# k of batch 0 in one transfer in place of two halves, in a fused attention and maxout feed-forward kernel

## The chip, the core and the metric

The kernel runs on one NeuronCore of a Trainium2 chip. The metric is the device time of one execution in microseconds (us); the median of several executions is compared. The core has five engines with instruction queues of their own: TensorE (PE, with its weight loads shown as PEld), VectorE (DVE), ScalarE (ACT), GpSimd (POOL) and SyncE (SP). Transfers between HBM and the on-chip memory run on 16 DMA engines that all queues share. A transfer that casts float32 to bfloat16 is issued by POOL here, and goes through one queue, which the profile calls software_dynamic.

## What is computed

For 8 batches and 8 heads, with sequence length 576, head size 64 and 32 memory slots:

```python
a = exp(phi - max over s); a = a / sum over s
k_m = einsum('bhsm,bhsd->bhmd', a, k)
v_m = einsum('bhsm,bhsd->bhmd', a, v)
scores = q @ k_m^T / 8
attn = softmax(scores)
x = (attn @ v_m), heads joined: 4608 x 512
h = maximum(maximum(x @ w1, x @ w2), x @ w3)     # 512 -> 768
out = h @ w_out                                  # 768 -> 512, float32
```

All inputs are float32 in HBM; the kernel computes in bfloat16.

## The kernel before

One batch is handled as four pairs of heads (index j, 0 to 3). A load of k, v or q of a batch puts 128 partitions x 4 pairs x 576 elements into a tile: 576 KB in bfloat16, 512 rows of 1152 bytes each, one for each partition and pair. The stages of a batch b are: the exponential of phi (E), the products of that with k and v over the sequence (B, L249, into PSUM), a normalization and transposition of the small result (N and K, L269 to L304), the scores against the transposed q (Q at L313, S at L333), the softmax, and then the feed-forward part. The feed-forward weights are folded with each batch's v_m (D, L440), so that the kernel multiplies the folded weights by the attention (F, L466), takes the maxima, and multiplies by w_out (T, L497 and L506). For that it once needs the product of w3 and w_out: W transposes w3 (L184), and O multiplies it by w_out (L192).

The order of everything is written out by hand, in one string of tokens (L594 on) that `issue` (L561) turns into calls: `X@b` is stage X of batch b. Each engine and each queue gets its instructions in the order of the string. The tokens that matter here:

- `E@0`: the two exponentials of batch 0, on ACT. Their input phi is loaded by SP in two transfers, ahead of the string (L91).
- `L1@b`, `L2@b`, `L3@b`: k, v, q of batch b, each in one transfer issued by POOL (L97 and L110). `L0@b`: phi of a later batch (L93).
- `H0@b` to `H3@b`: half of k or v, two pairs of heads in one transfer (L97 too). `H0` is k of pairs 0 and 1, `H2` k of pairs 2 and 3, `H1` and `H3` the same for v.
- `Y0@0` to `Y3@0`: the weights w1, w2, w3 (L116) and w_out (L123).
- `Z25@0`, `Z9@0`, `Z2@0`, `Z6@0`: so many matrix products on zeros (L159), whose results nobody reads.
- `B0@0`: the products with k of batch 0. Its 72 matmuls run over c (9 positions), j (4 pairs) and two heads, with c outermost, so the first eight read all four pairs.
- `B1@0`: the products with v of batch 0, read straight from the loaded tile.

POOL's transfers of batch 0 are issued in this order: k of pairs 2 and 3, k of pairs 0 and 1, q, w3, w_out, v in two halves, w1, w2; then phi, k, q and v of batch 1. The completion of POOL's transfers is counted on eight semaphores in rotation, so the ninth transfer is issued only when the first has landed, the tenth only when the second has, and so on: w2 waits for the first half of k, phi of batch 1 for the second half, k of batch 1 for q, q of batch 1 for w3, and v of batch 1 for w_out.

The load in question, with `h` the slice of the pairs:

```python
    def load_kv(b, i, h=slice(0, NP)):
        kv = loaded.setdefault(b, {})["kv"] = kvos[b % 2]
        nc.gpsimd.dma_start(
            out=kv[:, 1 - i, h].rearrange("p j c d -> p j (c d)"),
            in_=by_pair((k, v)[i], b)[:, h],
        )
```

Of the kernel before, what the change touches and what calls it, by code (L numbers as in the profile page):

```python
# [15 lines left out]
def kernel(  # L16
# [14 lines left out]
    B, H, S, D = q.shape  # L31
# [529 lines left out]
    def issue(b, n, swap):  # L561

        i = int(n[1:]) if len(n) > 1 else None
        {
            "I": lambda: [make_identity(nc, ident)]
            + [nc.gpsimd.memset(x[:, :, :, 2 * D : 2 * D + 1], 1.0) for x in kvrs],
            "Y": lambda: load_w(i) if i < 3 else load_wo(),
            "L": lambda: load_ph(b) if i == 0 else load_q(b) if i == 3 else load_kv(b, i - 1),
            "H": lambda: load_kv(b, i % 2, halves[i // 2]),
            "r": lambda: pack(b, i),  # L570
            "E": lambda: [att_exp(b, h) for h in (halves if b == 0 else [slice(0, NP)])],
            "B": lambda: att_kv(b, i),
            "N": lambda: att_kv_norm(b, i),
            "K": lambda: att_kv_t(b, swap, i),
            "Q": lambda: att_q(b, i),
            "S": lambda: att_score(b),
            "a": lambda: att_t(b, i),
            "s": lambda: att_sum(b, i),
            "c": lambda: att_rec(b, i),
            "m": lambda: att_mul(b, i),  # L580
            "X": lambda: (ones_mul if (b, i) in ONES else att_back)(b, i),
            "M": lambda: ones_sum(b, i),
            "R": lambda: ones_rec(b, i),
            "D": lambda: fold(b, i, swap),
            "F": lambda: ffn1(b, i, swap),
            "T": lambda: ffn2(b, i, swap),
            "W": lambda: w3_t(i, swap),
            "O": lambda: w3_o(i, swap),
            "V": lambda: w_diff(i),
            "Z": lambda: warm_up(i),  # L590
        }[n[0]]()


    for w in """  # L594
        E@0 H2@0 H0@0 L3@0 Z25@0 B0@0 I@0 N0@0 Z2@0 K0@0! Q0@0 Q1@0 Z9@0 S@0 Z2@0 M0@0 M1@0
        R0@0 Y2@0 R1@0 W0@0 Y3@0 W1@0 W2@0 Z6@0 O1@0 H3@0 O3@0 O2@0 H1@0 X1@0 B1@0 X0@0 N1@0
        K1@0 O0@0 Y0@0 D1@0! D0@0! D3@0 F8@0 F10@0 F2@0 V0@0 F6@0 F0@0! Y1@0 D2@0 D4@0 F4@0
        L0@1 V1@0 F1@0 E@1 F3@0 L1@1 F5@0 F9@0 F7@0 L3@1 F11@0 B0@1 T3@0 N0@1 K0@1! L2@1 Q1@1
        L2@2 L1@2 Q0@1 L0@2 V2@0 T0@0! L3@2 S@1 T1@0 a0@1 s0@1 c0@1 m0@1 B1@1 N1@1 a1@1 L1@3
        K1@1 s1@1 D0@1 D1@1! D2@1 c1@1 m1@1 X0@1 L3@3 r1@2 X1@1 T2@0! L2@3 F6@1 F10@1 F7@1 F2@1  # L600
        F3@1 F4@1 F0@1 r0@2 E@2 F5@1 F1@1 F11@1 L0@3 L0@4 F8@1 L2@4 F9@1 B@2 D3@1 N@2 Q1@2
        T0@1! K@2 T2@1! r0@3 Q0@2 S@2 a0@2 a1@2 s1@2 c1@2 m1@2 T4@1! D1@2! s0@2 D2@2 c0@2 m0@2
        X1@2 D0@2 T3@1 Q0@3 L3@4 X0@2 Q1@3 T1@1 F0@2 F4@2 F8@2 F6@2 F9@2 E@3 F7@2 r1@3 F5@2
        F10@2 F1@2 B@3 L1@4 D3@2 N@3 L0@5 F2@2 F11@2 E@4 F3@2 L1@5 K@3 r1@4 L2@5 T2@2! S@3 T3@2
        a0@3 s0@3 c0@3 m0@3 D0@3 D2@3 a1@3 s1@3 c1@3 X0@3 D1@3! Q0@4 m1@3 T1@2 L3@5 L2@6 T0@2!
        X1@3 F10@3 r0@4 F2@3 F4@3 E@5 Q1@4 r0@5 F5@3 F3@3 L1@6 F8@3 B@4 N@4 D3@3 F9@3 F6@3
        F11@3 L0@6 K@4 F0@3 F7@3 F1@3 S@4 a0@4 T4@3! s0@4 a1@4 D0@4 c0@4 s1@4 r1@5 c1@4 D3@4
        m0@4 X0@4 Q0@5 T0@3! D1@4! D2@4 B@5 T3@3 m1@4 X1@4 L0@7 F10@4 Q1@5 N@5 F8@4 K@5 F6@4
        F9@4 S@5 F7@4 L3@6 F2@4 F4@4 a0@5 L1@7 a1@5 F0@4 s0@5 r1@6 F3@4 D0@5 r0@6 s1@5 c1@5 E@6
        D3@5 m1@5 c0@5 F1@4 T1@3 L2@7 F11@4 L3@7 E@7 F5@4 m0@5 B@6 D1@5! D2@5 X1@5 N@6 T2@3!  # L610
        X0@5 F6@5 F8@5 Q0@6 Q1@6 K@6 F4@5 F9@5 S@6 F7@5 r0@7 a0@6 F2@5 a1@6 s0@6 c0@6 F0@5
        F10@5 m0@6 F1@5 s1@6 c1@6 F11@5 F5@5 T0@4! F3@5 X0@6 T2@4! r1@7 D0@6 D1@6! Q0@7 B@7
        m1@6 N@7 X1@6 T2@5! K@7 T3@4 Q1@7 S@7 a0@7 F2@6 s0@7 a1@7 s1@7 c1@7 m1@7 c0@7 F4@6
        T4@5! D3@6 D2@7 D0@7! T0@5! D3@7 D2@6 X1@7 m0@7 D1@7! T1@4 X0@7 F6@7 F3@6 T1@5 F4@7
        F8@7 F0@7 F5@6 F10@6 F7@7 F9@7 F10@7 F5@7 F0@6 F11@7 F6@6 F1@7 F7@6 F2@7 F8@6 F11@6
        F9@6 F1@6 F3@7 T0@6! T0@7! T3@5 T2@7! T2@6! T1@6 T1@7 T3@6 T4@7! T3@7
    """.split():
        n, b = w.rstrip("!").split("@")
        issue(int(b), n, w.endswith("!"))
# [30 lines left out]
```

## Time and profile before

| what | value |
|---|---|
| time, median of 3 runs | 165.75 us (165.37 to 166.11) |
| time of the profiled execution | 164.78 us |
| its span, first to last instruction | 163.0 us |
| PE busy | 152.5 us (94%) |
| ACT, DVE, POOL busy | 100.5, 90.3, 69.6 us |
| granted TensorE clock, mean | 0.998 |
| moved by the software_dynamic queue | 21.43 MB, 68.7% of 16 engines' span |
| two half loads of k, issue to landing | 7.0 us (median) |

The span is the time from the first to the last instruction of one profiled execution; about 1.8 us of the execution's own time lie around it. In the windows of the profile, "DMA share" is the mean busy share of the 16 DMA engines (it passes 1 where packets of one engine overlap), and GB/s is what they moved, counted in bytes at the destination. In the chain of waits, each piece is followed back to what released it, so a stretch marked DMA is one in which the end of the kernel hung on a transfer from its issue to its landing.

### The profile page before, as it was taken

How to read it: one execution, taken by the hardware profiler on the slowest of the kernel's cores; microseconds unless marked ns; L12 is line 12 of the kernel's file. 1: busy time of each engine (PE TensorE's matmuls, PEld its weight loads, DVE VectorE, ACT ScalarE, POOL GpSimd, SP SyncE). 2: the span in 40 equal slices, each digit the busy share in tenths (PEclk: the TensorE clock that was granted, in tenths of full speed). 3: DMA queues.
4: the chain of work that ended last, by engine and by line, in shares of the span. 5: the costliest groups of instructions: out<-in, count | busy, mean ns of one | idle time of the engine just before them, and what ended most of it. 6: DMA issues, size and time to landing. Idle time of an engine off the chain costs nothing.

```text
span 163.0 us, 4818 instructions
## 1 busy us (share of the span) xinstructions
PE 152.5 (94%) x2060; PEld 85.4 (52%) x2080; DVE 90.3 (55%) x181; ACT 100.5 (62%) x151; POOL 69.6 (43%) x71
## 2 busy tenths in 40 slices
PE   7968798999899999999999999999999999999990
PEld 2433444664377436744673575576553467744450
DVE  2013703898838575848499658879749128810010
ACT  4204435935497488778876899994558976223320
POOL 7931215100699268548849967656403100000000
PEclk9999999999999999999999999999999999999999
DMA  5999999999999999999999999997313130014333
GB/s 154 153 199 208 206 210 212 279 207 209 259 311 237 208 251 373 283 209 286 260 264 206 234 347 270 195 237 157 129 73 126 68 129 0 0 69 186 135 129 131
DMA packets 21974, 31.77 MB, mean 195 GB/s; under 512 B 1216, under 2 KB 16576, under 8 KB 21952
## 3 DMA queue, kind: packets, MB, share of 16 engines
q0 software_dynamic: 16080, 21.43, 68.7%
q1 hardware_dynamic: 5728, 9.90, 17.2%
q8 instruction: 16, 0.26, 0.6%
q10 hardware_dynamic: 144, 0.13, 0.2%
q14 instruction: 6, 0.05, 0.1%
HBM read 39.32 MB, written 9.44 MB: 299 GB/s over the span
## 4 chain that ended last, share of the span: by engine, by line
PE 83%; DMA 9%; POOL 2%; issue 1%; ACT 1%; DVE 1%; POOLq 0%; ACTq 0%
PE psum L466 30%; PE psum L497 28%; DMA wo_sb<-in_moe_w_out_dram 9%; PE psum L506 8%; PE psum L440 5%; PE psum L249 4%; PE psum L192 3%; PE psum L333 2%; PE psum L515 1%; POOL kvo L97 1%; PE psum L298 1%; PE psum L538 1%; POOL qq L110 0%; DVE kvn L273 0%; ACT w3o L172 0%
## 5 line engine op out<-in xcount | busy, mean ns | idle before, releaser
L497 PE MATMUL psum<-wo_sb,hT 128*128 128x512 bf16 x193 | 49.7, 380 | 1.4 <-issue 0.6
L466 PE MATMUL psum<-attn,wp 128*128 128x288 bf16 x384 | 50.5, 286 | 0.1
L479 DVE TENSOR_TENSOR hT<-psum,h 128x576 bf16<-128x576 f32 x48 | 34.2, 749 | 17.5 <-PE psum L466 12.0
L466 PEld LDWEIGHTS <-wp 128*128 128x128 bf16 x384 | 36.7, 98 | 13.2 <-issue 2.0
L172 ACT COPY ot<-psum 128x512 f32<-128x512 f32 x35 | 20.7, 591 | 32.2 <-PE psum L506 25.2
L497 PEld LDWEIGHTS <-hT 128*128 128x128 bf16 x210 | 19.2, 98 | 24.1 <-issue 4.3
L172 ACT CAST wp<-psum 128x1024 bf16<-128x1024 f32 (+1 forms) x31 | 29.3, 996 | 3.3 <-PE psum L440 1.5
L103 POOL COPY kvr<-kvo 128x2304 bf16<-128x2304 bf16 x12 | 25.4, 2116 | 13.7 <-DMA kvo<-in_k_dram 10.2
L170 ACT ACTIVATE h<-psum 128x576 bf16<-128x576 f32 x47 | 28.4, 660 | 3.5 <-PE psum L466 3.3
L409 POOL TENSOR_TENSOR t<-t,sm 128x576 bf16<-128x576 bf16 x14 | 16.1, 1156 | 24.6 <-DVE sm L404 24.5
L506 PE MATMUL psum<-wp,attn 128*128 128x512 bf16 x62 | 18.4, 379 | 0.0
L159 PE MATMUL psum<-warm 128*128 128x512 bf16 x42 | 12.0, 438 | 1.4 <-DVE warm L128 1.2
L313 DVE STREAM_TRANSPOSE qT<-qq 128x576 f32<-128x576 f32 x16 | 11.7, 746 | 1.2 <-DMA qq<-in_q_dram 1.1
L342 ACT ACTIVATE e<-psum 128x576 bf16<-128x576 f32 x16 | 9.6, 652 | 3.7 <-PE psum L333 3.7
L229 ACT ACTIVATE e<-ph 128x1152 bf16<-128x1152 f32 (+1 forms) x9 | 9.6, 1068 | 1.8 <-DMA ph<-in_phi_dram 1.7
L395 DVE TENSOR_REDUCE sm<-t 128x18 f32<-128x576 bf16 x14 | 10.3, 737 | 0.2
L387 DVE STREAM_TRANSPOSE t<-e 128x288 f32<-128x288 f32 x14 | 6.4, 464 | 6.3 <-ACT e L342 6.2
L97 POOL DMA_DIRECT2D kvo<-in_v_dram x9 | 6.7, 751 | 7.2 <-PE psum L249 4.1
L506 PEld LDWEIGHTS <-attn 128*128 128x128 bf16 x62 | 6.1, 98 | 7.1
L555 DVE COPY ot<-psum 128x256 f32<-128x256 f32 x1 | 0.4, 425 | 15.4 <-PE psum L546 15.4
L249 PEld LDWEIGHTS <-e 64*32 64x32 bf16 x720 | 6.9, 90 | 3.6 <-issue 3.2
L110 POOL DMA_DIRECT2D qq<-in_q_dram x8 | 6.2, 770 | 6.0 <-DMA w_sb<-in_moe_w_dram 6.0
(57 smaller groups left out, 114.4 us busy)
## 6 DMA issues: line engine op xcount, KB each, us to landing
out_dram<-ot SPq DMA_DIRECT2D x35, 256.0 KB, 5.5
qq<-in_q_dram POOLq DMA_DIRECT2D x8, 576.0 KB, 12.7
ph<-in_phi_dram POOLq DMA_DIRECT2D x7, 576.0 KB, 14.4
kvo<-in_k_dram POOLq DMA_DIRECT2D x7, 576.0 KB, 14.1
kvo<-in_v_dram POOLq DMA_DIRECT2D x7, 576.0 KB, 15.8
w_sb<-in_moe_w_dram POOLq DMA_DIRECT2D x3, 768.0 KB, 19.2
wo_sb<-in_moe_w_out_dram POOLq DMA_DIRECT2D x1, 768.0 KB, 14.9
ph<-in_phi_dram SPq DMA_DIRECT2D x2, 288.0 KB, 3.1
```

The source lines that it names most:

```text
L103: nc.gpsimd.tensor_copy(out=kvrs[b % 2][:, :, :, D * i : D * (i + 1)], in_=kvos[b % 2][:, 1 - i])
L159: nc.tensor.matmul(po[:, 0:BANK], lhsT=warm[:, 0:P], rhs=warm, start=True, stop=True)
L170: nc.scalar.activation(out=out_, in_=in_, func=AF.Relu)
L172: nc.scalar.copy(out=out_, in_=in_)
L249: nc.tensor.matmul(kvp[M * j : M * (j + 1), a, 0:nd], lhsT=s["e"][r, j, c, :], rhs={None: lambda: kvr[r, j, c, 0:nd], 0: lambda: k_and_one ...
L313: nc.vector.transpose(out=s["qT"][:, j].rearrange("p j c r e -> p (j c r e)").bitcast(FP32), in_=loaded[b]["q"][:, j].rearrange("p j c d - ...
L395: nc.vector.tensor_reduce(out=sm, in_=s["t", g].rearrange("p n r e -> p n e r"), op=ALU.add, axis=mybir.AxisListType.X,)
L409: nc.gpsimd.tensor_tensor(out=t, in0=t, in1=s["sm", g].unsqueeze(2).to_broadcast([P, S // HP, R, 2]), op=ALU.mult,)
L466: nc.tensor.matmul(acc[:, h, 0:SH], lhsT=wps[b][:, g, w * DF + ft * P : w * DF + (ft + 1) * P], rhs=attn[:, g, c0 : c0 + SH], start=(g == ...
L479: nc.vector.tensor_tensor(out=hT[:, ft, (b % 2) * S : (b % 2 + 1) * S].rearrange("p (h n) -> p h n", h=2), in0=a, in1=s["h1", ft], op=ALU.max,
L497: nc.tensor.matmul(po, lhsT=hT[:, fc, c0 : c0 + P], rhs=wo_sb[:, fc, :], start=(n == 0), stop=False,)
L506: nc.tensor.matmul(po, lhsT=attn[:, g, c0 : c0 + P], rhs=wp3s[b][:, g, :], start=False, stop=(g == NG - 1),)
```

## The change

One line of the string of tokens. The two half loads of k of batch 0 are replaced by the load of the whole, at the same place:

```diff
     for w in """
-        E@0 H2@0 H0@0 L3@0 Z25@0 B0@0 I@0 N0@0 Z2@0 K0@0! Q0@0 Q1@0 Z9@0 S@0 Z2@0 M0@0 M1@0
+        E@0 L1@0 L3@0 Z25@0 B0@0 I@0 N0@0 Z2@0 K0@0! Q0@0 Q1@0 Z9@0 S@0 Z2@0 M0@0 M1@0
         R0@0 Y2@0 R1@0 W0@0 Y3@0 W1@0 W2@0 Z6@0 O1@0 H3@0 O3@0 O2@0 H1@0 X1@0 B1@0 X0@0 N1@0
```

`L1@0` calls `load_kv(0, 0)` with all pairs, `H2@0` and `H0@0` called it with pairs 2 and 3, then 0 and 1. The same 512 rows go to the same places. POOL has one transfer fewer; the other engines have the same instructions in the same order. The rotation of the eight semaphores moves by one: w2 no longer waits for a landing, phi of batch 1 waits for the whole of k, and every later transfer waits for the same earlier transfer as before.

## The prediction

> **What bounds the kernel now.** I read the chain of waits first, in order of time, for the opening 30 us, since the change touches only the opening:
>
> ```profile
> 1.25 0.89 POOL kvo L97
> ...
> 2.15 0.70 POOL kvo L97
> 2.85 0.76 POOL qq L110
> ...
> 5.01 14.86 DMA wo_sb<-in_moe_w_out_dram
> ...
> 19.92 4.04 PE psum L192 x18
> ```
>
> The columns are start, length and what. Up to 19.9 us the end of the kernel hangs on w_out landing; it is issued at 5.01 and takes 14.86 us because it stands in the queue behind k, q and w3. Then PE takes over, and the whole-run shares of the chain (PE 83%, DMA 9%, the 9% being this one wait) say that it keeps the chain to the end. The timeline of PE shows what stands ahead of that point:
>
> ```profile
> 9.54 0.80 PE L249 MATMUL psum<-kvo,e 64*32 64x128 bf16 x72 [0.72 <-DMA kvo<-in_k_dram]
> ...
> 17.62 1.24 PE L159 MATMUL psum<-warm 128*128 128x512 bf16 x5
> 19.92 4.04 PE L192 MATMUL psum<-wo_sb,w3T 128*128 128x512 bf16 x18 [1.05 <-DMA wo_sb<-in_moe_w_out_dram]
> ```
>
> PE waits 0.72 us for k at 9.54, but that wait is not on the path: everything between 9.5 and 18.9 is filled with products on zeros, and PE then stands 1.05 us for w_out. So k may land a little earlier or later at no price. What counts is when the queue has brought w_out, and that is read from the stream of the DMA engines in windows of half a microsecond (the last three columns: granted clock, DMA share, GB/s):
>
> ```profile
> 3.50:4.00 0.50, 0.50 (x3) 0.15 (x1) 0.00 (x0) 0.28 (x1) 0.42 (x3) 1.00 1.12 334
> 4.00:4.50 0.50, 0.50 (x2) 0.15 (x1) 0.00 (x0) 0.43 (x2) 0.50 (x4) 1.00 1.18 173
> 4.50:5.00 0.50, 0.50 (x2) 0.15 (x1) 0.00 (x0) 0.50 (x1) 0.50 (x2) 1.00 0.95 159
> 5.00:5.50 0.50, 0.50 (x3) 0.23 (x2) 0.00 (x0) 0.15 (x1) 0.50 (x2) 1.00 1.29 143
> 5.50:6.00 0.50, 0.50 (x4) 0.22 (x3) 0.00 (x0) 0.00 (x0) 0.50 (x2) 1.00 0.76 81
> 6.00:6.50 0.50, 0.50 (x4) 0.20 (x2) 0.00 (x0) 0.00 (x0) 0.50 (x1) 1.00 0.97 122
> 6.50:7.00 0.50, 0.50 (x4) 0.26 (x3) 0.00 (x0) 0.00 (x0) 0.50 (x2) 1.00 1.09 175
> ...
> 8.00:8.50 0.50, 0.50 (x4) 0.20 (x2) 0.00 (x0) 0.00 (x0) 0.28 (x2) 1.00 1.14 168
> ```
>
> Until 4 us the stream is phi (uncast, 320 to 334 GB/s), then k. Between 5.0 and 6.5 it falls to 81 GB/s and recovers. The packet records of the trace place this: on most of the 16 engines the first half of k is through between 5.25 and 5.8, and the first packets of the second half take 0.3 to 1.3 us where the usual one takes 0.11. The dip lies on the seam between the two transfers that the change joins.
>
> **The change part by part.**
>
> POOL: two issues of 0.89 and 0.72 us (2.85 - 1.25 = 1.60 together) give way to one. What a whole load of k or v costs is in the rows of the same line:
>
> ```profile
> L97 POOL DMA_DIRECT2D kvo<-in_k_dram x4: 722/746/885, 1.2 to 25.7; - x4
> ```
>
> About 0.75 us, so q, the identity, w3, w_out and all up to w1 are issued some 0.85 us earlier. Worth nothing by itself: w_out is issued at 5.01 and its packets can start only when w3 is through, on the fastest engine at 14.3 by the packet records, so 9 us of backlog cover it. Were the cover gone, it would be worth its whole 0.85 us.
>
> The semaphore rotation: w2, issued at 8.26 after 0.22 us of waiting for the first half of k, waits for nothing and is issued about 1.1 us earlier. Its last packets come at 29.9, over 21 us after the issue, so this is worth nothing either. The next in POOL's queue, phi of batch 1, waits for the end of k as before; behind it stand the loads of batch 1, each waiting for the transfer it waited for before. If k lands earlier they follow, into a queue that has a backlog anyway.
>
> The seam: if the dip goes away, the whole stream behind it moves up. Take 170 GB/s as its undisturbed rate here (between the 159 and 173 ahead of the dip and the 175 behind it): the three windows from 5.0 to 6.5 miss 27, 89 and 48 GB/s over 0.5 us each, 82 KB, which at 170 GB/s is 0.48 us. By 159 GB/s they miss 65 KB, or 0.41 us. I take 0.45 us as the size of the dip. How much of it comes back? In the one whole transfer whose predecessors had nearly run dry (v of the last batch, issued at 101.85, its first packets at 103.9) there is a slack stretch too:
>
> ```profile
> 103.50:104.00 0.50, 0.50 (x17) 0.11 (x2) 0.50 (x2) 0.50 (x2) 0.50 (x1) 1.00 1.27 205
> 104.00:104.50 0.50, 0.45 (x3) 0.25 (x3) 0.47 (x4) 0.50 (x1) 0.50 (x1) 1.00 1.17 175
> ```
>
> So a seam behind which the next transfer was issued only 2 us earlier costs something (about 0.27 us there, 175, 171 and 171 GB/s in three windows against some 207 around them: 52 KB at 207, or 0.25 to 0.27 with 205 to 212). The seam from k to q, where q was issued 4.5 us ahead, shows only the 168 between 187 and 184 GB/s: under 0.06 us. After the change the seam from k to q is the only one left in the opening, with q issued at 2.0 and due at about 7.2, a lead of 5 us. I therefore let nearly all of the 0.45 us come back, and set 0.4.
>
> The start of the stream: the first packet of k starts at 3.60, 2.35 us after the issue of the half at 1.25. No row shows the start of a whole load on an idle queue, so it is bounded. From below: v of the last batch above had its first packets 2.1 us after its issue with no gap behind the transfer ahead of it, so twice the rows need not take longer; and the 3.60 is the moment at which the first DMA engine is done with phi, so an earlier readiness gains at most the share of phi's own bandwidth that k would take, which is nothing in sum. From above: if the first packet waits until all 512 rows are described, and the second 256 cost what the second issue cost, it starts 0.72 us later. I take the nearer row, 746 against 722 ns, which is 0.03 us later.
>
> The Trainium skill has two rules that pull apart here. "DMA: Bandwidth & Descriptors", section "Anatomy of one DMA - SWDGE (gpsimd) path", gives a fixed cost of about 2.0 us for each DMA; taken as serial, the change would gain 2.0 us, but the row of the seam has room for no more than 0.48, so most of a fixed cost is overlapped here. The same page, section "Queues, rings and completion order", says that a DMA engine takes turns between the queues it has work for, packet by packet; this speaks against the change, since by it k's packets would have mixed with phi's before 3.60 had they been ready, so that the start would hang on k's descriptors and not on phi, and a larger transfer could be late by the 0.72 us of the bound.
>
> The sum: -0.40 (seam) + 0.03 (start) + 0 (POOL) + 0 (rotation) = -0.37 us on w_out's landing. PE's wait of 1.05 us ahead of L192 has room for it (the third copy of w3T ends at 18.68, the last product on zeros at 18.86). Behind it v, w1 and w2 come from the same stream and move with it, and PE, which has hardly any idle time from there on, carries the shift to the end one for one. The profiled execution would go from 164.78 to 164.41 (span 163.0 to 162.6). The median of the runs is 0.97 us above the profiled execution; from 165.75 the same step gives 165.4.
>
> **The rivals.**
>
> - A, the forecast: the seam's dip goes, 0.2 to 0.6 us, 165.15 to 165.55. Chance 0.38. For it: the place of the dip. Against: the records show slow packets also on engines whose first half was late, which no seam explains.
> - B, the dip is not the seam's but the opening's (cold descriptors, phi and POOL's writes in the same time), and stays where it is. The change then does nothing on the path: 165.75, within 0.2. Chance 0.25. For it: the seam from q to w3 shows no slow packet at all.
> - C, slower: the start is late. One mechanism, at the head of the queue: all 512 rows must be described before the first packet goes. Price up to 0.72 us, and the dip's slow first packets then stay in the opening as well, so w_out lands up to 0.7 later and PE's wait of 1.05 grows to 1.75: 166.45; with 1.5 us, if cold descriptors cost double, 167.2. It decides when the first packet starts more than 0.4 us later than 3.60. Chance 0.22. Against it: the 2.1 us of the last v.
> - D, more than the dip: w_out counts as landed when the slowest of 16 engines is done, and the packet records have that one about 0.8 us behind the fifteenth already at the end of k. If that lag was made on the seam, the landing gains 0.8 more at first, cut off by PE's 1.05 us: 164.7 to 164.9. Chance 0.15.
>
> **How the numbers follow.** The measurement of this kernel can tell about 0.5% (0.83 us) from no change. Within 0.83 us lie nearly all of A (0.82 of it) and B (0.92), 0.40 of C and 0.2 of D: 0.31 + 0.23 + 0.09 + 0.03 = 0.66. Faster by more: 0.18 of A with the spread of the runs (0.07) and 0.8 of D (0.12): 0.19. Slower by more: 0.6 of C (0.13; the first issue of the program took 0.89 against 0.75 us, so a cold start costs more than the warm rows say) and the rest of B (0.02): 0.15. The predicted time is A's, 165.4. The range takes in D down to 164.6 and C up to 166.6, its bound of 0.72 us, with a tenth for the spread of the runs; A's own range is 165.15 to 165.55.
>
> **What would show it.** Right: the windows from 5.0 to 6.5 us hold near 160 to 175 GB/s, the first packet of k starts by about 3.65, q is issued at about 2.0, w_out lands at some 19.1 to 19.4 in place of 19.9, and PE's wait ahead of L192 shrinks to about 0.65. B: the dip stands at the same time inside the one transfer. C: the window from 4.0 to 4.5 is thin, and the wait ahead of L192 is above 1.05. D: the wait is nearly gone. The prediction is wrong as a whole if w_out's landing and the end do not move together.

## The result and the profile after

| | before | after |
|---|---|---|
| median of 11 runs each on one chip | 165.26 us (164.76 to 166.11) | 166.18 us (165.26 to 167.19) |
| ratio, 95% interval | | 1.0053 (1.0029 to 1.0078) |
| profiled execution, its span | 164.78, 163.0 us | 165.70, 163.9 us |

The change costs 0.92 us where a gain of 0.35 was forecast. A repeat on another chip (e8 below) gave 166.75 against 165.19, 1.0092 (1.0062 to 1.0122). Both intervals lie above 1, so the sign holds; the size differs between the two. One run of e14 (226 us at a granted clock of 0.66) and one of e16 (167.99 us) were in a slower state of the chip and are left out below.

The page of the changed kernel, first its engines' busy time and then the shares of the chain of waits by engine:

```profile
PE 153.8 (94%) x2080; PEld 85.3 (52%) x2080; DVE 90.4 (55%) x181; ACT 100.5 (61%) x151; POOL 68.8 (42%) x70
...
PE 66%; DMA 27%; POOL 3%; issue 1%; ACT 1%; ACTq 0%; POOLq 0%
```

PE has the same 2080 products in both kernels (the page of before lists 2060 of them, with 2080 weight loads; some records are missing from a trace, so PE's busy time is not compared). But the chain no longer stays on PE from 20 us on. In order of time (start, length, what) it now reads:

```profile
6.53 20.26 DMA w_sb<-in_moe_w_dram
27.39 23.77 DMA ph<-in_phi_dram
51.17 1.17 ACT e L229
52.39 0.81 PE psum L249 x70
```

It runs through two loads of the software queue to phi of batch 2 at 51 us. PE's timeline at the two waits the prediction spoke of:

```profile
9.94 0.80 PE L249 MATMUL psum<-kvo,e 64*32 64x128 bf16 x72 [1.54 <-DMA kvo<-in_k_dram]
...
20.25 4.04 PE L192 MATMUL psum<-wo_sb,w3T 128*128 128x512 bf16 x18 [0.97 <-DMA wo_sb<-in_moe_w_out_dram]
```

k came 0.40 us later (9.94 for 9.54), and L192 starts 0.33 us later (20.25 for 19.92). The bracket is the idle time just before the instruction. It shrank to 0.97 because PE's work ahead of it had moved too, so the start is what to compare, not the wait.

Laying the two traces of PE instruction by instruction on each other, the shift is +0.33 us from L192 to 51 us, +0.78 from L249 of batch 2 on, and +0.93 from 88 us to the end. The second step is phi of batch 2. ACT's timeline of the kernel before, then of the changed one:

```profile
49.85 1.17 ACT L229 ACTIVATE e<-ph 128x1152 bf16<-128x1152 f32 x1
```

```profile
51.17 1.16 ACT L229 ACTIVATE e<-ph 128x1152 bf16<-128x1152 f32 x1 [0.86 <-DMA ph<-in_phi_dram]
```

An exponential that showed no wait now waits 0.86 us for its input. So 0.93 = 0.33 (w_out) + 0.45 (phi of batch 2) + 0.15 at 88 us, where no view names what PE waited for.

The stream in windows of half a microsecond, changed kernel (the last two columns: share of the DMA engines, GB/s):

```profile
3.50:4.00 0.50, 0.50 (x3) 0.15 (x1) 0.00 (x0) 0.48 (x1) 0.50 (x4) 1.00 1.12 254
4.00:4.50 0.50, 0.50 (x2) 0.15 (x1) 0.00 (x0) 0.20 (x1) 0.50 (x2) 1.00 0.80 122
4.50:5.00 0.50, 0.50 (x3) 0.20 (x2) 0.00 (x0) 0.31 (x1) 0.50 (x1) 1.00 1.07 136
5.00:5.50 0.50, 0.50 (x4) 0.26 (x3) 0.00 (x0) 0.37 (x1) 0.50 (x2) 1.00 1.06 150
5.50:6.00 0.50, 0.50 (x4) 0.23 (x3) 0.00 (x0) 0.00 (x0) 0.50 (x2) 1.00 1.07 170
6.00:6.50 0.50, 0.50 (x4) 0.20 (x2) 0.00 (x0) 0.00 (x0) 0.50 (x1) 1.00 1.21 194
```

In this profile the hole at 5.5 to 6.5 (81 and 122 GB/s) is filled (170, 194). But 3.5 to 5.0 went from 334, 173, 159 to 254, 122, 136. And the hole does not belong to the two halves as such: e2 below, which loads k in the same two halves, shows hardly any.

```profile
5.00:5.50 0.50, 0.50 (x3) 0.22 (x2) 0.00 (x0) 0.24 (x1) 0.42 (x3) 1.00 1.18 171
5.50:6.00 0.50, 0.50 (x4) 0.26 (x3) 0.00 (x0) 0.00 (x0) 0.50 (x4) 1.00 1.13 150
6.00:6.50 0.50, 0.50 (x4) 0.21 (x3) 0.00 (x0) 0.00 (x0) 0.50 (x2) 1.00 1.08 152
```

In e4, halves too, these windows hold 150, 138 and 173 GB/s. A dip to 81 was seen in one profile of three.

None of these views says why w_out lands later. The trace also holds the sixteen increments of each transfer's semaphore, one from each DMA engine; the transfer has landed at the sixteenth. Worked out from those records, in us (first, mean and last of the sixteen, and last minus first):

| transfer | before: first, mean, last | spread | after: first, mean, last | spread |
|---|---|---|---|---|
| end of k | 7.32, 8.10, 9.41 | 2.10 | 7.20, 7.94, 9.81 | 2.61 |
| q | 10.91, 11.23, 12.29 | 1.38 | 10.28, 11.02, 12.72 | 2.45 |
| w3 | 14.63, 15.02, 16.02 | 1.38 | 14.20, 14.86, 16.43 | 2.23 |
| w_out | 18.43, 18.84, 19.88 | 1.45 | 17.99, 18.65, 20.21 | 2.22 |

In this pair of profiles the first engine is through w_out 0.44 us earlier, which is the size forecast for the dip; the mean is 0.19 earlier; the last is 0.33 later. L192 starts 0.04 us after the last increment in both. The last one's delay is all there at the end of k (0.40), and later transfers make up little of it.

Over more profiles only the last engine separates the kernels. With k whole, w_out's mean increment comes at 18.65, 18.75 and 19.13 (after, e1, e8) and its last at 20.21, 20.85 and 20.92; with halves the mean comes at 18.84, 18.67 and 18.74 (before, e2, e4) and the last at 19.88, 19.72 and 19.60.

### The profile page after: what moved, and what is told of

Its sections match the earlier page's. It is cut to its first block, busy times and chain, and to the rows that moved or that the text cites. A ratio compares the mean times of both kernels' runs of the same rounds, so it can differ in the third digit from the quotient of the medians.

```text
span 163.9 us, 4837 instructions
## 1 busy us (share of the span) xinstructions
PE 153.8 (94%) x2080; PEld 85.3 (52%) x2080; DVE 90.4 (55%) x181; ACT 100.5 (61%) x151; POOL 68.8 (42%) x70
## 4 chain that ended last, share of the span: by engine, by line
PE 66%; DMA 27%; POOL 3%; issue 1%; ACT 1%; ACTq 0%; POOLq 0%
PE psum L497 25%; PE psum L466 22%; DMA ph<-in_phi_dram 14%; DMA w_sb<-in_moe_w_dram 12%; PE psum L506 7%; PE psum L440 4%; PE psum L249 3%; PE psum L333 2%; PE psum L515 1%; POOL kvo L97 1%; PE psum L538 1%; ACT e L229 1%; PE psum L298 1%; POOL wo_sb L123 1%; POOL qq L110 0%
## 5 line engine op out<-in xcount | busy, mean ns | idle before, releaser
L497 PE MATMUL psum<-wo_sb,hT 128*128 128x512 bf16 x210 | 51.4, 380 | 0.2
L466 PEld LDWEIGHTS <-wp 128*128 128x128 bf16 x384 | 36.7, 98 | 13.2 <-issue 2.0
L249 PEld LDWEIGHTS <-e 64*32 64x32 bf16 x720 | 6.9, 90 | 4.9 <-issue 3.6
```

Source lines behind the costliest of these rows:

```text
L249: nc.tensor.matmul(kvp[M * j : M * (j + 1), a, 0:nd], lhsT=s["e"][r, j, c, :], rhs={None: lambda: kvr[r, j, c, 0:nd], 0: lambda: k_and_one ...
L466: nc.tensor.matmul(acc[:, h, 0:SH], lhsT=wps[b][:, g, w * DF + ft * P : w * DF + (ft + 1) * P], rhs=attn[:, g, c0 : c0 + SH], start=(g == ...
L497: nc.tensor.matmul(po, lhsT=hT[:, fc, c0 : c0 + P], rhs=wo_sb[:, fc, :], start=(n == 0), stop=False,)
```

## The experiments

Two starting theories. *Spread*: one large transfer at the head of the queue leaves the sixteen engines further apart, and the last one decides. Rivals: the earlier *issue* of all that follows, and *POOL* issuing behind k while k's rows are still being described. In the diffs only the head of the string of tokens is shown. "Spread" is last minus first increment, from one profile; ratios are to the kernel before on the same chip, with the 95% interval. e9 to e11, e15 and e17 have one run each, and stand in the text below.

| run | head of the queue | ratio | spread, end of k | spread, w_out | L192 starts |
|---|---|---|---|---|---|
| before | halves | 1 | 2.10 | 1.45 | 19.92 |
| after | whole | 1.0053 (1.0029 to 1.0078) | 2.61 | 2.22 | 20.25 |
| e8, after again | whole | 1.0092 (1.0062 to 1.0122) | 3.26 | 2.45 | 20.96 |
| e1 | whole, q late | 1.0077 (1.0047 to 1.0106) | 3.34 | 2.72 | 20.89 |
| e6 | tiny, then whole | 1.0044 (1.0015 to 1.0073) | 1.91 | 2.31 | 20.67 |
| e16 | whole, phi in the same queue | 1.0050 (1.0025 to 1.0074) | 2.00 | 1.39 | 20.57 |
| e5 | quarter, three quarters | 0.9994 (0.9967 to 1.0021) | 1.78 | 0.95 | 19.37 |
| e4 | halves, swapped | 0.9993 (0.9966 to 1.0021) | 1.33 | 1.46 | 19.64 |
| e2 | halves, w3 and w_out issued early | 0.9977 (0.9957 to 0.9996) | 1.94 | 1.58 | 19.76 |
| e3 | quarters | 0.9974 (0.9952 to 0.9996) | 0.86 | 1.69 | 19.75 |
| e7 | quarters, w3 and w_out issued early | 0.9973 (0.9951 to 0.9994) | 1.07 | 1.12 | 19.10 |
| e12 | pause of 5 memsets, whole | 1.0008 (0.9979 to 1.0036) | 0.91 | 1.80 | 20.48 |
| e13 | pause of 8 memsets, whole | 1.0010 (0.9985 to 1.0035) | 0.39 | 1.12 | 19.92 |
| e14 | pause of 8 memsets, halves | 1.0074 (1.0049 to 1.0099) | 0.77 | 1.04 | 20.41 |

### e1 and e2: is it the issue times?

e1 puts three POOL memsets behind the one transfer, so that q and all behind it are issued when they were before; e2 keeps the halves and issues w3 and w_out early.

```diff
-        E@0 H2@0 H0@0 L3@0 Z25@0 B0@0 I@0
+        E@0 L1@0 P@0 L3@0 Z25@0 B0@0 I@0                   # e1
+        E@0 H2@0 H0@0 L3@0 Y2@0 Y3@0 Z25@0 B0@0 I@0        # e2
+            "P": lambda: [nc.gpsimd.memset(kvrs[1][:, 0, 0, 0:P], 0.0) for _ in range(3)],
```

> k of batch 0 stays one transfer, but POOL then fills about 0.7 us with three small memsets ahead of q, so q, w3, w_out and all later issues come at the times that they had with two halves. Theory 1 (the size of the first transfer sets how unevenly the 16 engines start; the last engine lags by over 2 us and w_out counts as landed only with it): still slower than before, ratio 1.003 to 1.007, w_out's first and last increments about 2.2 us apart, PE starts on w_out at about 20.2. Theory 2 (the loss comes from POOL writing the later transfers 0.7 us earlier, while k runs): the same as before, ratio 0.998 to 1.002, increments about 1.4 us apart, PE starts at about 19.9.

> Two halves of k as before, but w3 and w_out are issued ahead of the identity and the small memsets, about 0.7 us earlier. Theory 1 (size of the first transfer): nothing, ratio 0.998 to 1.002, w_out's increments about 1.4 us apart. Theory 2 (earlier issues disturb k): slower, ratio 1.003 to 1.007, increments about 2.2 us apart.

Timeline of POOL, e1 (start, length):

```profile
1.24 0.93 POOL L97 DMA_DIRECT2D kvo<-in_k_dram  x1 [0.80 <-POOLq L635]
2.17 0.75 POOL L570 MEMSET kvr<- 128x128 bf16 x3
2.87 0.75 POOL L110 DMA_DIRECT2D qq<-in_q_dram  x1
```

q is issued at 2.87 as before the change (2.85), and the loss is still there: 166.34 against 165.12 us, and the trace of PE:

```profile
20.89 4.04 PE L192 MATMUL psum<-wo_sb,w3T 128*128 128x512 bf16 x18 [0.52 <-DMA wo_sb<-in_moe_w_out_dram]
```

w_out's first engine is done at 18.13, its last at 20.85; the ratio of 1.0077 is a little above what was expected. e2, with w3 and w_out issued as early as in the changed kernel (3.59 and 4.32 us against 3.57 and 4.33), is if anything faster than before (164.86). Issue times are not the cause.

### e3, e4, e7: smaller pieces

```diff
-        E@0 H2@0 H0@0 L3@0 Z25@0 B0@0 I@0
+        E@0 G3@0 G2@0 G1@0 G0@0 L3@0 Z25@0 B0@0 I@0              # e3
+        E@0 H0@0 H2@0 L3@0 Z25@0 B0@0 I@0                        # e4
+        E@0 G3@0 G2@0 G1@0 G0@0 L3@0 Y2@0 Y3@0 Z25@0 B0@0 I@0    # e7
+            "G": lambda: load_kv(b, 0, slice(i, i + 1)),
```

> k of batch 0 in four transfers, one for each pair of heads. Theory 1 (a smaller first transfer lets the engines start more evenly, each seam costs the early ones): the first increments of w_out come later than before (over 18.4), the spread to the last is at most 1.4 us, ratio 0.996 to 1.002. Theory 2 (issue times; all later issues come 1.4 us later than before): 0.996 to 1.000. Theory 3 (more transfers cost more at each seam, 0.45 us each, for all engines): 1.004 to 1.007, PE starts on w_out at about 20.8.

> Two halves of k, with pairs 0 and 1 first and pairs 2 and 3 second, as the one transfer has them. Theory 1 and 2: nothing, ratio 0.998 to 1.002. Theory 4 (what the change really loses is the order in which the pairs are read): slower, 1.003 to 1.007, the spread of w_out's increments as in the one transfer, about 2.2 us.

> k in four transfers, and w3 and w_out issued ahead of the identity. Both edits alone took 0.2 to 0.3% off. Theory 1: the early issue does nothing, since the queue has a backlog, and the quarters do all: ratio 0.996 to 0.999. If both gains are real and add up: 0.993 to 0.996, PE starts on w_out at about 19.5.

Quarters have three seams where halves have one, and by the forecast's own step should have been slower. They are 0.26% faster (164.77 us; the interval ends just under 1), and k ends with a spread of 0.86. w_out's is 1.69, above the 1.4 that was expected; the last section says what came between. Which half goes first does not matter (e4). In e7 L192 starts earliest of all runs:

```profile
19.10 4.04 PE L192 MATMUL psum<-wo_sb,w3T 128*128 128x512 bf16 x18 [0.98 <-DMA wo_sb<-in_moe_w_out_dram]
```

That is 0.82 us before the kernel before, yet the ratio, 0.9973, is that of e3 (0.9974), and not the 0.993 to 0.996 of two gains that add up. Laid on the trace of before, e7's PE is 0.82 us ahead until 27 us, 0.52 from 30 and 0.22 from 39 us to the end: an earlier start is given back at later waits. e3 and e7 beat both kernels, the one before by 0.35 and 0.46 us.

### e5, e6, e8: is it the first transfer alone?

```diff
-        E@0 H2@0 H0@0 L3@0 Z25@0
+        E@0 G3@0 J@0 L3@0 Z25@0      # e5: J is pairs 0 to 2 in one transfer
+        E@0 P@0 L1@0 L3@0 Z25@0      # e6: P loads 128 rows of 128 bytes that nobody reads
+        E@0 L1@0 L3@0 Z25@0          # e8: the changed kernel again
```

> k of batch 0 in two transfers again, but a quarter (pair 3) and then the other three pairs. Theory 1a (one or a few of the 16 engines run at about half speed for as long as the first transfer of the queue lasts, so the lag grows with the size of the first transfer): the lag at the end of the first transfer is about 0.9 us as with quarters and does not grow in the second, w_out's increments spread over less than 1.5 us, ratio 0.995 to 0.999. Theory 1b (every large transfer in the cold opening starts unevenly, whether it is the first or not): the second transfer, of three quarters, adds its own lag, the spread of k is over 2 us, ratio 1.002 to 1.006.

> The change (k in one transfer) with one small transfer ahead of it, 128 rows of 128 bytes, whose result nobody reads. Theory 1a (the first transfer of the queue alone is uneven): the lag is made on the small one and is small, the spread of w_out's increments is under 1.6 us, ratio 0.995 to 1.001. Theory 1b (the size of the large transfer counts): as the change, spread over 2 us, ratio 1.003 to 1.008, plus 0.7 us of POOL's time that is covered.

> The change itself once more, for a second trace of the lag. Theory 1: the lag of the last engine belongs to the one transfer and comes again: the spread of k's increments is 2.4 to 3.4 us, that of w_out's over 2 us, ratio 1.003 to 1.008. Chance (the lag of that one profile was an accident, and the slowdown has another cause): the spread of w_out's increments is about 1.4 to 1.6 us, with the ratio still at 1.003 to 1.008.

If only the very first transfer suffered, a tiny one ahead should have taken the blame. It ended with a spread of 0.30, and the whole k behind it still with 1.91 and a ratio of 1.0044. So that variant falls: a large transfer in the opening is uneven also when it is not the first. e6 has as many transfers as the kernel before, so its semaphores rotate as there, and it still loses: the rotation is not the cause either. With a quarter ahead (e5) the rest of k ended at 1.78, but w_out at 0.95 and the ratio is 0.9994. Its profile was 0.6 us slower than its median, by a wait of 1.3 us for k of batch 1 at 34 us. The spread at the end of k orders the kernels roughly, not exactly.

### e9, e10, e11: POOL, the pause and k itself

e9 puts eight memsets (2.04 us) ahead of k, e10 puts them between k and q, e11 loads q ahead of k, each whole.

```diff
-        E@0 H2@0 H0@0 L3@0 Z25@0
+        E@0 P@0 L1@0 L3@0 Z25@0      # e9
+        E@0 L1@0 P@0 L3@0 Z25@0      # e10
+        E@0 L3@0 L1@0 Z25@0          # e11
```

> The change with about 1.9 us of small memsets on POOL ahead of the load of k, so that phi is through before k's packets begin. The question is the lag and not the time, which grows by up to 1.9 us. Theory 1b-size (a large transfer into the empty queue is uneven whatever runs beside it): spread of k's increments 2.4 to 3.4 us as in the change. Theory 1b-phi (the unevenness comes from phi's transfers on the other queue, which end at different times on the 16 engines): spread under 1.5 us.

> The change with about 1.9 us of small memsets on POOL behind the load of k and ahead of q, so that POOL issues no transfer between 2.2 and 4.1 us, while k's first packets run. Theory 1b-size: spread of k's increments 2.4 to 3.4 us. Theory 5 (POOL's issue of the transfers behind k slows some engines while k runs): under 1.9 us.

> q whole and then k whole. Theory 1b-size: the first large transfer is uneven, whichever it is: q's increments spread over 2.4 to 3.4 us at its end, and k's behind it do not grow beyond that. Theory 6 (something about k's own rows): q's spread is under 1.5 us. The time grows by some 2 us in both, since k lands 3 us later and the scores behind it come after w_out.

One run each, beside 165.97 us for before. e10, whose next transfer is not issued until 4.17 us, ends with a spread of 2.99 at k and 2.11 at w_out, L192 at 20.49; its single time of 165.50 us decides nothing. So POOL's later issues are not the cause. In e11 it is q, then first, that ends with 2.37, so the rows of k are not special; L192 came at 22.17 and the time was 167.25, but there k is a whole transfer later too, and with it the products ahead of L192. e9 was the surprise: k was issued 1.5 us later, and its spread fell to 0.46 (165.38 us, with L192 at 19.94).

### e12 to e15: the pause, timed

e12 is e9 with five memsets (k issued at 1.93), e13 is e9 again, e14 has the halves behind the same pause, and e15 adds six VectorE memsets (2.06 to 6.28 us), since VectorE's own memsets (0.86 to 1.89 us) are over when a paused k starts, and nearer to it in the changed kernel.

```diff
-        E@0 H2@0 H0@0 L3@0 Z25@0
+        E@0 P@0 L1@0 L3@0 Z25@0            # e12, e13, e15
+        E@0 P@0 H2@0 H0@0 L3@0 Z25@0       # e14
+    for _ in range(6):
+        nc.vector.memset(kvrs[1][:, 1], 0.0)    # e15
```

> The change with about 1.3 us of small memsets on POOL ahead of k, so that k is issued at about 2.0: after VectorE's memsets (they end at 1.9), but its packets would be ready at about 3.6, before phi is through at 4.1 to 4.5. Theory P (phi's tail): the spread of k's increments is 2 to 3.4 us as in the change, ratio 1.003 to 1.010. Theory V (VectorE's memsets): under 1 us, GB/s near 200 from 5 us on, ratio 0.993 to 0.999.

> The 2 us of memsets ahead of k once more, now timed. Both theories: the spread of k's increments is under 1 us and that of w_out's under 1.3, PE starts on w_out at 19.6 to 20.0, ratio 0.996 to 1.001.

> The 2 us of memsets ahead of the two halves of the kernel before. If the change loses only by the disturbed opening, halves have no advantage here: spread of k's increments under 1 us, PE starts on w_out within 0.3 us of the whole's start, ratio within 0.2% of the whole's. If the one transfer is worse by itself, halves are faster than the whole by 0.4 to 0.9% here too.

> The 2 us of memsets ahead of k, with six more memsets on VectorE (128 x 1170 bf16 each) from 1.9 to some 4.5 us, so that VectorE is at work while POOL writes k's descriptors. Theory V: the lag is back, spread of k's increments over 2 us. Theory P: it stays under 1 us.

The windows of e13, then of e14 (last column GB/s):

```profile
5.00:5.50 0.50, 0.50 (x3) 0.21 (x2) 0.00 (x0) 0.18 (x1) 0.50 (x3) 1.00 0.58 81
5.50:6.00 0.50, 0.50 (x4) 0.26 (x3) 0.00 (x0) 0.00 (x0) 0.50 (x2) 1.00 1.17 200
6.00:6.50 0.50, 0.50 (x4) 0.21 (x3) 0.00 (x0) 0.00 (x0) 0.50 (x1) 1.00 1.23 212
...
8.00:8.50 0.50, 0.50 (x4) 0.19 (x2) 0.00 (x0) 0.00 (x0) 0.50 (x2) 1.00 1.16 194
8.50:9.00 0.50, 0.50 (x28) 0.18 (x33) 0.00 (x0) 0.00 (x0) 0.50 (x2) 1.00 1.26 217
```

```profile
5.00:5.50 0.50, 0.50 (x3) 0.22 (x2) 0.00 (x0) 0.31 (x1) 0.42 (x3) 1.00 0.93 141
5.50:6.00 0.50, 0.50 (x3) 0.22 (x2) 0.00 (x0) 0.00 (x0) 0.50 (x4) 1.00 1.45 180
6.00:6.50 0.50, 0.50 (x3) 0.16 (x2) 0.00 (x0) 0.00 (x0) 0.50 (x3) 1.00 0.86 129
...
8.00:8.50 0.50, 0.50 (x4) 0.26 (x3) 0.00 (x0) 0.00 (x0) 0.50 (x2) 1.00 1.06 138
8.50:9.00 0.50, 0.50 (x4) 0.22 (x3) 0.00 (x0) 0.00 (x0) 0.50 (x2) 1.00 1.02 173
```

In e13 k finds the engines free: phi's last packet ends at 4.09, the first packet of k starts at 4.37, and from 5.5 us on the stream holds 194 to 217 GB/s without a break. The halves show the dip at their seam (129) and one more where q begins (138, 173). With the engines level the forecast's sign is right: 165.39 us for the whole, 166.13 for the halves, which neither expectation of e14 had. But the seam between the halves is not where the difference arises: the halves begin to flow earlier (141 against 81 GB/s from 5.0 to 5.5), k's mean increment is the same (8.42 and 8.44), and the 0.50 us appears at q (mean 11.28 and 11.78), whose issue the second half had put off from 3.64 to 4.31. That the late issue costs this is argued, not shown; e10, with q at 4.17, has a slow q too (mean 7.72 to 11.38, where e13 takes 2.86). The pause itself costs the whole about what the level engines gain: 1.0010. VectorE's writes did nothing (e15: spread 0.67 at k, 1.08 at w_out, 165.20 us in one run).

e12 missed what was expected of phi's tail: 0.91 in place of 2 to 3.4. By that expectation it spoke for VectorE, which e15 then ruled out. Its k began while phi still ran (first packet of k at 3.83, last of phi done at 4.20), just as in e8 (3.85 and 4.18), which ended with 3.26. So phi's tail alone does not make the lag.

### e16, e17: what must stand ahead of k?

e16 lets POOL issue phi of batch 0 too, in k's queue, with no pause. e17 is e13 with two loads of 256 KB on SP's queue behind phi, which nobody reads.

```diff
-                nc.sync.dma_start(out=dst[:, h], in_=by_pair(phi, b)[:, h])
+                nc.gpsimd.dma_start(out=dst[:, h], in_=by_pair(phi, b)[:, h])       # e16
+    for i in range(2):                                                              # e17
+        ot = opool.tile([P, DM], FP32, name="ot")
+        nc.sync.dma_start(out=ot, in_=moe_w_out[P * i : P * (i + 1), :])
```

> The change with phi of batch 0 issued by POOL, ahead of k, in the same queue; nothing runs on the other queue, and the first issue stays at 1.25. Theory P (k stands ready while another queue is served): no second queue, so no unevenness: spread of k's increments under 1 us, 200 GB/s while k runs. Theory A (what is issued at 1.2 to 2.0 is uneven): phi's increments spread over 1.5 us already and k's too. Time: phi lands about 0.7 us later and k with it, so by P w_out lands at 19.4 to 20.0 and the ratio is 0.995 to 1.001, by A 1.005 to 1.012.

> The 2 us pause ahead of k as before, but SP issues two more loads behind phi (256 KB each, read by nobody), so that the other queue is busy until about 5.7 us, while k stands ready from 4.3 on. Theory P: the unevenness is back, spread of k's increments over 1.8 us. Theory A: it stays under 1 us, and k is only later, by up to 1.4 us.

e17: the same late k, but with the engines at work for another queue until 5.4 to 6.7 us, ends with a spread of 2.43 again (0.39 in e13), w_out at 2.59 and 167.33 us in one run. The sixteen engines end each of its two extra loads some 1.33 us apart already, so part of the 2.43 may be theirs. e16 gave 2.00 for k, with phi's own spreads at 0.60 and 0.58, and fell between the two expectations: to judge by this profile, a second queue is not needed.

## Why the prediction was wrong

**The step that failed** is the seam term in the sum of the landing: "-0.40 (seam) + 0.03 (start) ... = -0.37 us on w_out's landing". The landing came 0.33 us later, and 0.97 and 1.04 later in e1 and e8. Two things in the term were wrong.

- It took the mean of the stream for the landing. A transfer has landed when the last of sixteen engines is done, and the term that moves that one was missing. Rival D had looked at the right thing, the lag of the last engine, and gave it the wrong sign: the lag was not made on the seam, it is less with a seam. In the increments of before, the second half of k took the last engine 1.43 us (7.98 to 9.41) and the mean of the sixteen 2.08; in e2 it was 1.43 and 1.74, in e4 1.44 and 1.77. So at a seam most engines lose time, the last one loses least and comes closer: the spread fell from 2.40 to 2.10, 2.06 to 1.94 and 1.64 to 1.33 from the first half to the second. The dip was mostly time lost by engines that nobody waited for. (That the last is the same engine throughout is inferred; the records do not name it.)
- The size of the dip, 82 KB, was read from one profile and put down to the seam. By the same reading e2's windows miss 19 KB, with the same seam. As a gain of the mean it was -0.16 at the end of k and -0.19 at w_out in the pair of profiles above, and at w_out -0.09 in e1 and +0.29 in e8. In that pair the rest stayed in the opening, as B had it, moved to 3.5 to 5.0 us.

**Point by point.** POOL's earlier issue at nothing: right, by e1 and e2 (in e1 the loss stands with the old issue times); the one issue took 0.93 us where 0.75 was taken from the median of its line, so q came 0.68 us earlier and not 0.85. The rotation at nothing: right, by e6. The start: right, first packet between 3.5 and 3.6 in both (3.85 in e8), and on free engines 1.66 us after the issue for the whole (e13), 1.60 for a half (e14). So C, which gave the sign and almost the size (166.45), falls by its own condition; the thin window from 4.0 to 4.5 that was to mark C appeared without it. PE's start on w_out as the point from which the shift runs: right, +0.33 held for 30 us. "One for one to the end": wrong. More than half of the loss, 0.45 + 0.15 us, came later, the 0.45 at a wait for the same queue. In e8 the shift grew at 67 us (phi of batch 3, +1.04 to +1.46) and at 95 us (to +1.97), where the chain runs through POOL's copy of a k that landed 2.3 us later than in before (86.00 against 83.70). In e7 a gain shrank. PE's 94% hid how near those waits were, and the timeline, which marks waits alone, did not show it. The increments of before do: phi of batch 2 landed at 49.73, 0.12 us ahead of the exponential at 49.85, so there was next to nothing in hand.

**The rules that bear on it.** The Trainium skill, "DMA: Bandwidth & Descriptors", section "Rules for kernel authors", asks for transfers of 1 MiB and more for the most bandwidth, and for one transfer in place of two to disjoint halves of the partitions. The halves here are halves of the pairs, each on all 128 partitions, and k is 576 KB, so neither rule names this case. What they would suggest, the larger transfer, came out better with the engines level (1.0010 in e13 against 1.0074 in e14) and worse in this kernel's opening (1.0053, and quarters 0.9974). The same page, section "Why a DMA increments its semaphore by 16 and not by 1", says that the sixteen engines finish independently and that only the full count means landed. The table of increments agrees, and this was the rule to weigh.

The turn-taking between queues, which the prediction set against the change, did not show at the start of k. In e13 the first packet came 1.66 us after the issue (2.71 to 4.37), so k issued at 1.24 would be ready at about 2.9 (an estimate from that row); its first packet came at 3.5 to 3.6, with the first engine free of phi.

**What is shown and what stays open.** Shown: PE starts on w_out when the last engine is done (0.04 us behind it in both profiles), and in this opening the last engine is later when k is whole: k ends with a spread of 1.9 to 3.3 us whole (after, e1, e6, e8, e10), 1.3 to 2.1 in halves (before, e2, e4) and 0.9 to 1.1 in quarters (e3, e7), and w_out lands after 20.2 us in all the first and before 19.9 in all the others. On engines that are done with phi a whole k ends with 0.4 to 0.7 (e9, e13, e15). Open: why the engines drift apart within such a transfer. Other loads still running on the engines go with it (e16 and e17 too, 2.0 and 2.4), but are not enough, since e12 had them and ended with 0.91. Open too: why the later transfers, q to w2, which stand ready as well, add nothing in e1 and e8. The link from spread to time is not exact either: e12 and e16 have L192 at 20.48 and 20.57 in their profiles, but ratios of 1.0008 and 1.0050, and e14 has small spreads and 1.0074.

## What to carry to other kernels

Cost a transfer by its last DMA engine, not by the mean of the stream: a dip in GB/s may be time of engines that nobody waits for, and filling it then gains nothing. Look for such a dip in a second profile before giving it a price. Smaller pieces of the first load let the late engine catch up in this opening, and cost nothing there (behind a pause, in e14, they did). Look at what the next loads in the same queue have in hand, in the increments, before carrying a shift one for one.

## What the hardware showed that was not expected

- What is left at w_out of a lag made at k stays. In e1 the spread is 2.98 at q, 2.72 at w_out and 2.72 still at the load of q of batch 1, which lands at 38 us, through ten transfers at full stream. Between k and w_out it can shrink (before 2.10 to 1.45, e5 1.78 to 0.95).
- Fetching instructions takes time of the DMA engines. Part 3 of the changed kernel's page (packets, MB, share of 16 engines):

```profile
q8 instruction: 16, 0.26, 0.6%
```

  Sixteen packets of 16 KB; 0.6% of 16 engines over 163.9 us is 15.7 us, nearly 1 us each. In the records they take 0.9 to 1.1 us mostly, at 14.0, 27.9, 34.1, 40.3 and 47.3 us and on. It shows best where the engines are level: in e13 q ends with a spread of 0.40, a packet of 0.94 us starts at 13.2, and w3's fifteenth increment comes at 15.19 and its last at 16.06. The same stands in e3, e9 and e12, so part of w_out's spread there was not made at k. Where a packet falls on an engine that is late already, the landing can move: k of batch 1 in e5 had its fifteenth increment at 34.13 and its last at 35.56, with one at 33.5. phi of batch 2 had a spread of 1.73 before and 3.9 after; both kernels have a packet in that stretch (46.7 and 47.3), so how much of the 0.45 us is the lag's and how much chance is open. Which engine took the packet isn't recorded, so this is a coincidence in time, seen several times, and no run removed it.
